# Attention and two MoE layers on one core: the third pair of heads of the first chunk through fp16 halves and DMA transposes, with a new order table

## The chip, the cores and the metric

The kernel runs on one core of one Trainium2 chip. The metric is the device time of the launch in microseconds (us), as a median over runs; lower is better. The five engines are named as the profile names them: PE is the matrix engine (PEld its weight loads), DVE the vector engine, ACT the scalar engine, POOL the GpSimd engine, SP the engine that issues most DMAs.

## What is computed

Attention with a hash mask, then two feed-forward layers, all in float32 at the interface. Batch 2, 8 heads, 768 positions, head size 64; the layers see 1536 tokens of width 512.

```python
def _attn_ref(q, k, v, proj):
    q_bits = (einsum(q, proj) > 0); k_bits = (einsum(k, proj) > 0)      # 6 bits -> a bucket
    mask = q_bucket[:, :, :, None] == k_bucket[:, :, None, :]
    scores = where(mask, scale * q @ k^T, -1e9)
    attn = exp(scores - max); attn = attn / (sum(attn) + 1e-09)
    return attn @ v
def _moe_ref(x, w1, w2, w3, w_out):      # d_ff 768
    return max(x @ w1, x @ w2, x @ w3) @ w_out
def _moe2_ref(x, w_in, w_out):           # d_ff 2048
    h = x @ w_in; g = where(h > 0, h, exp(min(h, 0)) - 1)
    return g @ w_out
```

## The kernel before

**Tiles.** The work is cut into six chunks of 256 tokens (c = 0 to 5; three for each batch), each chunk into four pairs of heads. A pair of a chunk is numbered u = 4c + p (24 of them), and is four tiles t = 4u to 4u + 3 (96 in all): two heads by two blocks of 128 queries, each against all 768 keys. For each tile `plan_tile` makes, in this chain: scores on PE (L621, four matmuls into one of the two PSUM tiles `s`), the row maximum on DVE (L624), two tiny DVE steps that make `scale` and `bias` (L625, L627), and the exponential on ACT into the float32 tile `P` (L629). Then P has to be transposed and multiplied with V, and there are two ways:

- **float32 path**, `if u < FU` with FU = 4, so all four pairs of chunk 0 (16 tiles). PE transposes P in six blocks back into the same `s` tile (L641, `turn32`), ACT copies that to SBUF (L645; the table may also give it to DVE), and PE multiplies in float32 with the raw V (L650, `pv32`; twelve matmul records for a tile). The row sum comes from the exponential itself, with an accumulate read behind it on ACT.
- **fp16 path**, all other pairs (80 tiles). P is split into two fp16 halves: a cast (L658 on ACT or L660 on DVE), the rest by a subtraction on POOL or DVE (L664), both into `hl`. SP issues a DMA transpose of twelve 128x128 blocks into `PT` (L666), and PE multiplies with V split likewise (L672 to L674, 18 matmuls). The row sum is a column of ones in V.

When the four tiles of a pair are done, L690 to L697 normalise them into `xn`, and after every second pair SP transposes `xn` into `xT` (L700), the input of the chunk's first layer.

**What else runs early.** `plan_qk` prepares q and k (load, norm, scaling L396 and L397, a split L398 and L400, PE transposes L410, copies to `qa`/`ka` L413, DMA copies to `qb`/`kb` L417, hash bits L429 to L464), `plan_v` prepares V, and `plan_w13` the weights of the first layer: loads into the three buffers `raww` (L531), conversions on ACT and DVE (L535, L539 or L540, L543 or L544, L546), a norm and a split (L558 to L560). The raw V of batch 0 lies in the space of `wot`, the second weight of the first layer; so `wot` is written after the last float32 product of chunk 0. The first layer (`plan_moe1`, L713) of a chunk starts when its `xT` is there; chunk 0's is the first large block of matmuls, and its second half (L713 with `wot`) needs the whole of the first half. The second layer (L713 with `win`, L848) follows.

**The order.** Nothing is scheduled at build time. `ORDER` is a packed table that lists all operations in one sequence with the engine of each; where an operation has two possible engines (a cast on ACT or DVE, a subtraction on POOL or DVE, a DMA issued from SP or ACT), the table chooses. Each engine carries out its own operations in that sequence, and waits at the head of it. Buffers of a ring are handed out in the same sequence.

Of the kernel before, what the change touches and what calls it, by code (L numbers as in the profile page):

```python
# [30 lines left out]
class Graph:  # L31
# [73 lines left out]
    "c-lQyOITXx))u_6@y5m*8*gm9vC$at$|h<6O~OWvfLG8cV48~QKx_wMG7y`A*bKyzf!Gejb|AI`@pK@z1F;>5?LbTiVmlB|2I9#;Ob3#a|9Sqk&H4Yezi)l-`>uDb4UgNcWz6SqKV$!(5=mvVN=j#N"  # L105
    "UYZxbaC_pfyb0VH#K#-Q{hL!L@yD)|EQI>ufz@F1o3Y)KSzPaUb6yn;&OCQ6#%A5uPUiA=F1Li6?m6)kt}A@s`|GDDxx3zQy0__k`*)Pktj44}ISg~}>3gp*<Qw!iGxo@|sC-`@Q!JXP_>nHIxOP*_"
    "Roys4;5BgO2-XzyrGa()oa>XK<R4~Lxc8|EI}ljad@;UnBlI%6^yj&H^Wo2!Qu8#Vo)4?^$Ajj`nQkc>NxwSwYa@oM^Xr)5<jv$~%S=CJet`#PhOHjtEoUn5s|h=ro!;|W@x8w$dEq%b?pO%!FK+mj"
    "jf9(3>+yuV&Mn`%EOrszj_*Z&R52#^FqUg;o{R3!U?F@3f8jFCi@%xwT^e?~E`Ih{CB%yjw?`r;HWya+13O+)9Xi;FD%7^{*}KR~Dzc`~z0$Q`gmw)Rp)0fPa^eU3kMZ}D_9eH>G2==2O1Y#N_D(NQ"
    "{-3qR1fAm-<E+zVUNIRQJF5tSPPn6-#a_?GyKM}!e7MHlfvrioIT+fb7@H?ZU;;hWJ?C4mt+orZpp1;$ncFtw<+JpFSRDMFm<%bcClb6`T6JbmVE&tOIQ7WV(BJ3^3sVZe4L;_e;zK$1Lmh4ttHao-"
    "?r68UmJ`Jd5!Ibqk(n2qpcb^!_PJO{WD|xB&z72xH_uRW#4X{!u*Rp5W&E4f8O9g07oIP#7ffC+xv8jq=kr^acNEcp?ZA$IKzVx}bx8c%OI$vGqMMu}V&*?wYf|r}L+&<DM?P$L3|k4#^*LqdKUC`Y"  # L110
    "{DrS$g0ZmfUqt+i+(2&}^Bu$z74DgD#;K##F{AER+s2=p>|=v#-C~b8u$?yx*XB~+p`P)I`60@6ZT@PlKKlANwu2oEBH@2du+YeN=Letr&-wlUH;DYAeSWkWGf3WFGxwJni70YLoJ;WqvPvm8Cs;jG"
    "u9Nyp<;=gltn?Wl6^ifdeu*02vV!7uJ}P)A(XeJqi3u4z0^vneY%W~2oeerJS9F}c=>N=zH>AIj2xYE4vu<PW7XQGVE{q5WKln*m?V!@Fx3x#tf+}KW)lk>zF?oNSQ^n-I!*lP1ukA;FLhM4ecN}+r"
# [861 lines left out]
```

## Time and profile before

| | |
|---|---|
| three runs | 646.3, 646.44, 650.33 us; median 646.44 |
| the profiled execution | 646.06 us, of which 644.3 us from the first to the last instruction |
| mean granted clock of PE | 0.997 of full speed |
| busy, share of the span | PE 97%, DVE 82%, ACT 71%, POOL 34% |
| DMA | 81.35 MB, mean 126 GB/s |

The profile is one execution. Busy shares are averages over stages with different limits: the first 140 us (attention of chunk 0, preparing of weights, the first layer of chunk 0) look otherwise than the rest, so the stretches are read one by one. A row of the timeline has the start, the duration, the engine, the line, the operation and its tiles, and in brackets the idle time before it with what ended that. A matmul's row lasts from its issue to the modelled end of its pipeline; the next may start long before that, so the step from start to start is what it takes of PE.

### The profile page before, as it was taken

What the parts mean: (1) busy time and instruction counts of PE and PEld (TensorE: products, weight loads), DVE (VectorE), ACT (ScalarE), POOL (GpSimd) and SP (SyncE); (2) the same over time, 40 slices, a digit from 0 to 9 for tenths busy, and PEclk for the clock granted to TensorE, in tenths of its full rate; (3) what the DMA queues carried; (4) which work ended last, traced back from release to release, by engine and by line L of the source; (5) the groups of instructions that cost most, each with busy time, mean ns of one, the idle gap of its engine ahead of it and who ended that gap; (6) DMA issues with size and microseconds to landing.
All of it is one profiled execution on the core that took longest, in us unless ns stands there. A gap on an engine that the chain in (4) does not pass through costs nothing.

```text
span 644.3 us, 16489 instructions
## 1 busy us (share of the span) xinstructions
PE 624.7 (97%) x6414; PEld 490.8 (76%) x6414; DVE 528.0 (82%) x1493; ACT 454.8 (71%) x858; POOL 218.5 (34%) x196
## 2 busy tenths in 40 slices
PE   4999889999999999999999999999999999999997
PEld 4788768888888888888888887766676666667664
DVE  6899999998878988898765898888888676887564
ACT  3899999999878777866635878866755665554431
POOL 1210175756656474575631101112111221120021
PEclk9999989999999999999999999999999999999999
DMA  8775699979799777888666634231302100000022
GB/s 261 200 242 152 180 202 229 217 131 218 150 189 178 149 156 164 174 169 151 147 132 218 181 96 128 68 99 35 97 19 71 45 1 2 1 1 2 1 92 105
DMA packets 176030, 81.35 MB, mean 126 GB/s; under 512 B 142672, under 2 KB 170320, under 8 KB 175952
## 3 DMA queue, kind: packets, MB, share of 16 engines
q1 hardware_dynamic: 171678, 75.54, 50.3%
q10 hardware_dynamic: 4274, 4.76, 2.6%
q8 instruction: 50, 0.82, 0.6%
q14 instruction: 28, 0.23, 0.1%
HBM read 38.80 MB, written 3.15 MB: 65 GB/s over the span
## 4 chain that ended last, share of the span: by engine, by line
PE 80%; DVE 4%; ACT 4%; DMA 3%; issue 1%; POOL 0%; DVEq 0%; SPq 0%; ACTq 0%
PE mo L713 47%; PE out L848 19%; PE s L621 6%; PE o L672 2%; PE o L673 2%; PE o L674 2%; ACT P L629 1%; DVE m L624 1%; DMA kb<-ka 1%; DMA rawv<-in_v_dram 1%; PE mo L410 1%; DMA PT<-hl 1%; ACT hl L645 1%; DVE hx L734 0%; ACT mo L535 0%
## 5 line engine op out<-in xcount | busy, mean ns | idle before, releaser
L713 PE MATMUL mo<-xT,w 128*128 128x256 f16 x1296 | 152.6, 272 | 0.0
L664 POOL TENSOR_TENSOR hl<-P,hl 128x768 f16<-128x768 f32 x69 | 115.0, 1674 | 64.9 <-ACT hl L658 31.5
L713 PEld LDWEIGHTS <-w 128*128 128x128 f16 x1296 | 123.6, 98 | 16.7
L713 PE MATMUL mo<-x1T,win 128*128 128x256 f16 x1152 | 135.8, 273 | 0.0
L848 PE MATMUL out<-wo2t,gt 128*128 128x512 f16 x576 | 134.9, 379 | 0.0
L713 PEld LDWEIGHTS <-win 128*128 128x128 f16 x1152 | 112.3, 98 | 24.2
L629 ACT ACTIVATE P<-s,bias,scale 128x768 f32<-128x768 f32 x96 | 94.6, 991 | 28.8 <-DVE bias L627 17.6
L841 POOL TENSOR_TENSOR gt<-g,gt 128x256 f16<-128x256 f32 x57 | 39.3, 695 | 213.2 <-ACT gt L839 125.4
L624 DVE TENSOR_REDUCE m<-s 128x1 f32<-128x768 f32 x96 | 91.1, 951 | 12.6 <-PE s L621 11.2
L848 PEld LDWEIGHTS <-gt 128*128 128x128 f16 x576 | 54.9, 97 | 52.7
L832 ACT ACTIVATE r<-mo,nih 128x256 f32<-128x256 f32 x96 | 44.8, 469 | 69.1 <-PE mo L713 65.0
L835 DVE TENSOR_SCALAR uu<-e,sg 128x256 f32<-128x256 f32 x96 | 35.5, 371 | 26.3 <-ACT e L834 25.7
L658 ACT CAST hl<-P 128x768 f16<-128x768 f32 x62 | 50.7, 830 | 2.9 <-DMA PT<-hl 2.4
L672 PE MATMUL o<-vt,PT 128*128 128x65 f16 x480 | 51.3, 193 | 0.2
L673 PE MATMUL o<-vt,PT 128*128 128x64 f16 x480 | 51.3, 194 | 0.0
L674 PE MATMUL o<-vt,PT 128*128 128x65 f16 x480 | 51.1, 192 | 0.0
L837 DVE SCALAR_TENSOR_TENSOR g<-mo,aj,uu 128x256 f32<-128x256 f32 x96 | 46.1, 482 | 6.0 <-POOL gt L841 2.0
L621 PE MATMUL s<-ka,qa 128*128 128x384 f16 x192 | 48.1, 332 | 2.5 <-ACT P L629 1.9
L621 PE MATMUL s<-kb,qb 76*128 76x384 f16 x192 | 48.2, 332 | 1.0 <-DMA kb<-ka 1.0
L672 PEld LDWEIGHTS <-PT 128*128 128x128 f16 x480 | 44.4, 96 | 2.7 <-DMA PT<-hl 0.4
L673 PEld LDWEIGHTS <-PT 128*128 128x128 f16 x480 | 44.3, 97 | 2.1
L713 PEld LDWEIGHTS <-wot 128*128 128x128 f16 x432 | 41.4, 98 | 5.6
(212 smaller groups left out, 1158.7 us busy)
## 6 DMA issues: line engine op xcount, KB each, us to landing
raww<-in_moe_w_dram SPq DMA_DIRECT2D x17, 512.0 KB
raw<-in_moe_w_in_dram SPq DMA_DIRECT2D x14, 512.0 KB
raw<-in_moe_w_out_dram SPq DMA_DIRECT2D x13, 512.0 KB
rawk<-in_k_dram SPq DMA_DIRECT2D x8, 384.0 KB
raww<-in_moe_w_out_dram SPq DMA_DIRECT2D x6, 512.0 KB
out_dram<-ot SPq DMA_DIRECT2D x12, 256.0 KB
rawq<-in_q_dram SPq DMA_DIRECT2D x10, 256.0 KB
wot<-in_v_dram SPq DMA_DIRECT2D x4, 384.0 KB
```

What stands on the lines that cost most here:

```text
L621: PE.matmul(ps.ap[:, h, :NK], lh[0:n, h0 + i, j], rh[0:n, i, h * CH:(h + 1) * CH], start=first, stop=not first)
L624: op({"V": vred(S)}, lambda e: V.tensor_reduce(out=m.ap, in_=ps.ap[:, :, :NK], op=ALU.max, axis=AX.XY), rd=[ps], wr=[m], prio=t + 80.5)
L629: op({"A": act(S, ap=2, acc=int(u < FU)) - 42}, lambda e: A.activation(out=P.ap.rearrange("p (c n) -> p c n", c=2), in_=ps.ap[:, :, :NK], ...
L658: A.copy(hl.ap[:, 0], P.ap)
L664: op({"G": gtt(S), "V": (vtt(S), -109.46)}, lambda e: eng[e].tensor_tensor(out=hl.ap[:, 1], in0=P.ap, in1=hl.ap[:, 0], op=ALU.subtract), r ...
L672: PE.matmul(oo, pt.ap[:, kt], vt.ap[:, i, kt, :D + 1], start=(kt == 0), stop=False)
L673: PE.matmul(oo[:, :D], pt.ap[:, kt], vt.ap[:, i, kt, D + 2:], start=False, stop=False)
L674: PE.matmul(oo, pt.ap[:, NS + kt], vt.ap[:, i, kt, :D + 1], start=False, stop=(kt == NS - 1))
L713: PE.matmul(o, lh(kk, x), rh(kk, y), start=(kk == 0 and pi == 0), stop=(kk == n - 1 and pi == 2))
L832: op({"A": act(NQ, ap=1) - 42}, lambda e, m=m, o=o, r=r: A.activation(out=r.ap, in_=o.ap[:, :NQ], func=AF.Relu, scale=nih.ap[:, m:m + 1]), ...
L837: op({"V": vstt(NQ)}, lambda e, m=m, o=o, uu=uu, gg=gg: V.scalar_tensor_tensor(out=gg.ap, in0=o.ap[:, :NQ], scalar=aj.ap[:, m:m + 1], in1= ...
L848: PE.matmul(outs[j].ap, gt.ap[:, x, j * 128:(j + 1) * 128], wo2t[f].ap[:, y], start=(len(seen) == 1 and pi == 0), stop=(len(seen) == n and ...
```

## The change

The tiles of u = 2 (t = 8 to 11, the third pair of chunk 0) go by the fp16 path; u = 0, 1 and 3 stay in float32. Every `u < FU` becomes `u in FS`. The cost entries of three DMA operations change by a unit or take other numbers; `emit` does not read them. ORDER is a new table, for 3363 operations where there were 3359.

```diff
 ORDER = (
-    "c-lQyOITXx))u_6@y5m*8*gm9vC$at$|h<6O~OWvfLG8cV48~QKx_wMG7y`A*bKyzf!Gejb
...
+    "c-l2qOI#Xv*A~2SQ@LpvyfJuVP$M8JU^If42pR=M19)S+Bx1S{zjq<F3$a}U+lAOH#C9Pz3
...
-FU = 4
+FS = (0,1,3,)
...
-            if u < FU:
+            if u in FS:
                 plan_tile.zs = tn(UL, "zs", 2)
...
-        pt = ring(at, [128, 2 * NS, 128], "PT", 4, F16, True) if u >= FU else None
+        pt = ring(at, [128, 2 * NS, 128], "PT", 4, F16, True) if u not in FS else None
...
-            **(dict(accum_out=zs.ap[:, j * 2 + i:j * 2 + i + 1]) if u < FU else {})),
-           rd=[ps, sc, bi], wr=[P] + ([zs] if u < FU else []), prio=t + -196.32)
+            **(dict(accum_out=zs.ap[:, j * 2 + i:j * 2 + i + 1]) if u in FS else {})),
+           rd=[ps, sc, bi], wr=[P] + ([zs] if u in FS else []), prio=t + -196.32)
...
-        if u < FU:
+        if u in FS:
...
             def turn32(e):
...
-        if u >= FU:
+        if u not in FS:
             op({"A": act(S), "V": (vcopy(S), 337.62)}, hi, rd=[P], wr=[hl], two=True, prio=t + 53.24)
...
-        if u >= FU:
+        if u not in FS:
             attn_ops.append(op({"PE": 3 * pe(NS, D + 1)}, pv, rd=[pt, vt], wr=[o], prio=t + 7.27 + -25.59))
```

What the new table does with u = 2 shows on three engines. First ACT, at the tiles of u = 2. Before, two exponentials (with their row sums `zs`) and two copies of the transposed tile, with weight work (`dc2w`, `w`) between:

```order
L629 ACTIVATE P_1238,zs_1114<-s_1179,bias_1221,scale_1211 128x768
L558 ACTIVATE w_100<-dc2w_1029,swm 128x512
L543 ACTIVATE dc2w_1133<-raww_927 128x512
L629 ACTIVATE P_1261,zs_1114<-s_1205,bias_1252,scale_1247 128x768
L645 COPY hl_1268<-s_1179 128x768
L539 ACTIVATE dc2w_1277<-raww_1146 128x512
L645 COPY hl_1288<-s_1205 128x768
```

Now, at the same place:

```order
L629 ACTIVATE P_1123<-s_1075,bias_1102,scale_1089 128x768
L535 ACTIVATE mo_1127<-raww_1053 128x512
L629 ACTIVATE P_1132<-s_1084,bias_1116,scale_1114 128x768
L535 ACTIVATE mo_1146<-raww_1121 128x512
L658 CAST hl_1148<-P_1132 128x768
L413 COPY qa_1040<-mo_1039 128x1024
L629 ACTIVATE P_1181<-s_1135,bias_1144,scale_1142 128x768
```

The copies L645 are gone there, and of the four casts two stand on ACT (L658) and two on DVE (L660). Next POOL, from its third subtraction of k on. Before:

```order
L400 TENSOR_TENSOR natk_525<-rawk_247,natk_525 128x12x64
L400 TENSOR_TENSOR natq_646<-rawq_425,natq_646 128x8x64
L400 TENSOR_TENSOR natk_757<-rawk_416,natk_757 128x12x64
L400 TENSOR_TENSOR natq_1201<-rawq_764,natq_1201 128x8x64
L400 TENSOR_TENSOR natk_1286<-rawk_651,natk_1286 128x12x64
L697 TENSOR_TENSOR xn_1315<-xf_957,xn_1315 128x256
L697 TENSOR_TENSOR xn_1315<-xf_1216,xn_1315 128x256
```

Now:

```order
L400 TENSOR_TENSOR natk_693<-rawk_460,natk_693 128x12x64
L400 TENSOR_TENSOR natq_804<-rawq_517,natq_804 128x8x64
L400 TENSOR_TENSOR natq_1073<-rawq_960,natq_1073 128x8x64
L664 TENSOR_TENSOR hl_1125<-P_1123,hl_1125 128x768
L664 TENSOR_TENSOR hl_1148<-P_1132,hl_1148 128x768
L664 TENSOR_TENSOR hl_1214<-P_1181,hl_1214 128x768
L664 TENSOR_TENSOR hl_1239<-P_1237,hl_1239 128x768
L697 TENSOR_TENSOR xn_1217<-xf_987,xn_1217 128x256
L697 TENSOR_TENSOR xn_1217<-xf_1226,xn_1217 128x256
```

All four subtractions of u = 2 stand on POOL, ahead of the first `xn`; a k subtraction has left this place. Last SP, whose queue holds the loads of q, k and the weights and the copies to `kb` and `qb`. Before, from the copy of the fourth pair's keys on:

```order
L417 DMA kb3_845<-ka3_844 64x1536
L388 DMA rawq0_1235<-in_q_dram 128x4x128
L531 DMA raww1_1263<-in_moe_w3_dram 128x4x256
L464 DMA qb0_1050<-btq0_1177 12x8x128
L531 DMA raww0_1303<-in_moe_w1_dram 128x4x256
L388 DMA rawk0_1317<-in_k_dram 128x2x384
L531 DMA raww2_1391<-in_moe_w2_dram 128x4x256
L700 DMA_TRANSPOSE xT0_1407<-xn0_1315 128x8x128
```

Now, from the same copy on:

```order
L417 DMA kb3_758<-ka3_757 64x1536
L388 DMA rawq0_1192<-in_q_dram 128x4x128
L666 DMA_TRANSPOSE PT0_1199<-hl1_1125 128x12x128
L666 DMA_TRANSPOSE PT1_1234<-hl2_1148 128x12x128
L531 DMA raww2_1251<-in_moe_w1_dram 128x4x256
L666 DMA_TRANSPOSE PT2_1262<-hl0_1214 128x12x128
L666 DMA_TRANSPOSE PT3_1311<-hl1_1239 128x12x128
L531 DMA raww0_1426<-in_moe_w2_dram 128x4x256
L417 DMA qb0_1041<-qa0_1040 64x1024
L531 DMA raww1_1445<-in_moe_w2_dram 128x4x256
L464 DMA qb0_1041<-btq0_1406 12x8x128
```

Four transposes stand among the weight loads, and the loads of the fifth block of w1, w2 and w3 come behind them.

## Rows read from the trace of the kernel before

**Rows 1.** The page: span, busy time of PE, the chain by engine.

```profile
span 644.3 us, 16489 instructions
PE 624.7 (97%) x6414; PEld 490.8 (76%) x6414; DVE 528.0 (82%) x1493; ACT 454.8 (71%) x858; POOL 218.5 (34%) x196
PE 80%; DVE 4%; ACT 4%; DMA 3%; issue 1%; POOL 0%; DVEq 0%; SPq 0%; ACTq 0%
```

**Rows 2.** Stretches: length, busy us (instructions) by engine; PE clock, DMA share, GB/s.

```profile
40.00:60.00 20.00, 19.74 (x227) 17.74 (x226) 19.91 (x60) 20.00 (x37) 0.00 (x0) 1.00 0.60 182
60.00:80.00 20.00, 17.42 (x154) 14.95 (x152) 18.85 (x55) 19.22 (x37) 4.27 (x4) 1.00 0.65 177
80.00:100.00 20.00, 18.11 (x177) 14.50 (x175) 19.43 (x49) 19.87 (x29) 11.94 (x9) 0.91 0.96 193
100.00:120.00 20.00, 20.00 (x271) 16.94 (x267) 19.81 (x55) 20.00 (x32) 13.92 (x9) 1.00 1.05 237
0.00:139.50 139.50, 124.36 (x1479) 105.58 (x1480) 128.02 (x367) 125.81 (x214) 52.00 (x50) 0.99 0.83 206
139.50:640.50 501.00, 500.38 (x4937) 385.23 (x4934) 399.20 (x1126) 328.98 (x645) 166.46 (x146) 1.00 0.45 104
```

**Rows 3.** Timeline, PE: chunk 0's first product with wot.

```profile
139.51 0.82 PE L713 MATMUL mo<-hTa,wot 128*128 128x256 f16 x6
```

**Rows 4.** Timeline, PE: a float32 tile's transposes, its product, and what follows each.

```profile
56.81 0.87 PE L641 MATMUL s<-ident,P 128*128 128x128 f32 x6
57.52 0.22 PE L445 MATMUL mo<-ident,bitsq 128*96 128x128 f16 x1
...
58.23 1.45 PE L650 MATMUL o<-wot,hl 128*128 128x64 f32 x12
59.51 0.17 PE L280 MATMUL mo<-gm,ones 128*128 128x1 bf16 x1
```

**Rows 5.** Timeline, PE: first of 18 products of an fp16 tile, and what follows.

```profile
96.14 0.19 PE L672 MATMUL o<-vt,PT 128*128 128x65 f16 x1
...
96.68 0.49 PE L713 MATMUL mo<-xT,w 128*128 128x256 f16 x3
```

**Rows 6.** Groups by line: count, busy us, mean ns of one, idle before.

```profile
L645 ACT COPY hl<-s 128x768 f32<-128x768 f32 x16 | 12.6, 798 | 0.7 <-PE mo L281 0.7
L629 ACT ACTIVATION_READ_ACCUMULATOR P<-s,bias,scale 128x1 f32 x16 | 3.2, 203 | 0.0
L658 ACT CAST hl<-P 128x768 f16<-128x768 f32 x62 | 50.7, 830 | 2.9 <-DMA PT<-hl 2.4
L660 DVE CAST hl<-P 128x768 f16<-128x768 f32 x18 | 10.6, 588 | 0.1
L664 POOL TENSOR_TENSOR hl<-P,hl 128x768 f16<-128x768 f32 x69 | 115.0, 1674 | 64.9 <-ACT hl L658 31.5 <-DVE hl L660 18.0 <-issue 7.1
```

**Rows 7.** Timeline, DVE at the head: the first key norm.

```profile
7.31 0.29 DVE L301 TENSOR_REDUCE gm<-mo 128x1 f32<-128x128 f32 x1 [1.02 <-PE mo L297]
```

**Rows 8.** Tile PT: issue time on SP, min/median/max ns, first and last start.

```profile
L666 SPq DMA_TRANSPOSE PT<-hl x80: 1352/1414/3116, 86.2 to 329.3; - x80
```

**Rows 9.** Waits from 40 to 92 us: total, times, longest.

```profile
DVE dc2w L540 <- DMA raww<-in_moe_w_dram: 0.7, 1, 0.7
```

**Rows 10.** The chain in order of time: start, us, what.

```profile
60.60 6.27 DMA kb<-ka
```

**Rows 11.** Timeline: a DVE scaling that starts inside a POOL subtraction, and one alone.

```profile
80.33 0.42 DVE L398 TENSOR_SCALAR natq<-rawq 128x512 f16<-128x512 f32 x1
...
223.33 1.15 POOL L770 TENSOR_TENSOR x1T<-hx,x1T 128x512 f16<-128x512 f32 x1
...
223.49 1.28 DVE L398 TENSOR_SCALAR natq<-rawq 128x512 f16<-128x512 f32 x1
```

**Rows 12.** Stretches around the one fall of the granted clock.

```profile
85.00:86.00 1.00, 0.00 (x0) 0.00 (x0) 1.00 (x2) 1.00 (x3) 1.00 (x1) 1.00 0.57 121
86.60:90.00 3.40, 3.31 (x27) 2.40 (x27) 3.26 (x7) 3.37 (x5) 2.68 (x3) 0.53 1.15 210
```

More of the change, by code (lines that the diff above doesn't have):

```diff
@@ L109 @@
[L109 to L112, printed above, removed]
@@ new lines @@
+    "GV2e#dmU^;r;?adsn(`YSq95*-msxyesSM1dvtvEavtBdFCge;@Q;1>XUmDon=`W28)luy6T-+VOm`+_EVz}PHJo%?AW^OQeEt^Q`u4eekK_+<H-m9A9+M{mhmix-Y>@tU^6<BoDXrUe!W5AC0tfoQ"
+    "Ag1uKWfi8dNWD_!I$QIV+K)fK>1@%GjCkP8W<QM?Iw_Y9)?XT}aVFthw4BbHUL*}M3+Z}g0binib{zfr^g_R9`F1si#6xe7Y`FQrZi>uYZ`{~tqhx28=bA&;{_wf4kmP@Te*g2go<-(rBJc*;41BVD"
+    "HFR*e^A{SrrN}Ya7v6}%cM+ZOGj=qjgfDWjn>>iG`V17mTgZPAU>!yf^jGxlS9>9L=)D-zTX6e|>^vToDCZNucpGP5b|%|=Sj%rOv{ujj=X<NZn9bg1AXELEBQrka*Ujs{vj5b18gT4I3S3q^g-W(N"
+    "u=%k)$HKBVzBJE7?9Tlofn^;%#dLltuGEOXSW@v~XdL^(l(>~HAFDi3!_E6QDc09sDUIBM+jR~{mu2sC#~#Du2Wn>GcKL%>@3S*~jw=7sXJOH?l)UpPqEri_pE9sL-TAL^=@(PqCY1COu7jpIHT)!r"
@@ new lines @@
+    "vCdTv#o(_K2XR@aGqH4wy249(O;SWw`)6d@6|KcdLKas(9LM{1dEN~h?VFtkF4}d-y|V5POC#ICA#5tRun^+7&ZsW8?Qn^G^{?2n=jfHgyZYxwM1e*VvH7*q?+Sdft5u)cwHe)HiUY~*RKHfW6x=dc"
+    "L$;TQVE*sd-D4>BLr}IKSwg1lhia80W_8|po|Avxeh~?>kk+w(ed+NozU_YZ_Q+`G`EJmY&Fi0|;n>#F8HxqANmQ2f^W*4c;-55fEV@HkR>kMO_TK18)cvcOYu4_M-(u1wT}0hQQQ0X@%ZCu(6?O~Q"
+    "2Zt+aN5pV@#`K*3EJEf>OmRGs8exdY0((L7P`WHtUPLi9*|k2W(^vf-R9V#KKmT5*SeZCWsxuBs=C;;$9k|Oq;h|yh0WJ7LYYGJ24<B<dV_;29u`eA2Yd6A?f=yp{p+dmgIEcA?ZOHai^y0;*zgX}a"
+    ")c;x&_jtVGz2AJ>B<vIY)f)@E_U~_W)H7UfIX@u3+j4x<eHE5XIeGCkoRau}&Tg@$8{62JB5*@mlnOq>+{e+_%vi)pb5K;w>ytl_ufOe-#+itwOJNjXDLc|@<VR&#Gp#?3!FT)fzju=@I>W8`Q&h8^"
@@ new lines @@
+    "id&|FA^Z(RH{%Q+q9?9X7G|0;qZc2RE*WRe^}cHa6-$2K7JHavdiRi0nleQllC7*doa$-ULgQac<Q4Zi%eA$?>eCwiy8&LoH$j>8fBfOd;et@b4IT5M7jy1|=yuG}@{+>(^2502%4K_feM8a(|9tfx"
+    "edl#=ewL*E;vq$3I~xd<E%;<jS+&L7MNs|BVTkoXWSKe$`y!Y=<%dW#CR56Eh&g)Y7h-J_Z_TRGsZRXYF}uStzgXMqaJrTh3yRZL<b_)O<|KBy@}*v2aqh<OsfBnvmPo`6mf7pXKVE$GcH6z)jeW5s"
+    "Rd(-hPydgf6r|6acV8|~zr@qLs}7$g6n>=(!G6f>J3)3sL*dBzitrl|W$R4Jz4+|aO+f!=a^~{yv)`pYc<%my)8*EsIIkCYD^%}~`%KzjMz`n4i+pF>7-XLX(a`H7Ot#58M6pN<?{q6R!9&s7=x^_0"
+    "S7A*0gK8#;k*J*yj#crgs2R7bjQ_?Qvg@Ss=Iy)In4{ag-4bWrlC_4kd5djM{p+IUOS|jZwzj`1wL6@F;QEq3Uyt7|cD@XKZKP-qXM#>U+GRS5tUkBd|CP$v_4$uo?wkLtEQwP72!)4U2KFM-Go|<I"
@@ L153 @@
+    "YPAjzj#%#isl{d+g!2v-A{reW9UU4Pg6kt`vknao5y{ZtFu@L6M+b*Shix|75J3|G4#Ds+sD_EdhFfjJ0371s;gKPHa2OxNho23P4dWvt&xVHZk)h$yu`%1|<S>p8kKk}X1B8P(jt`CDV`KREI8OMn"
+    ";o%`0PT(#ZA15vxw@rM^$Hqp+?&$IHkqO|&CML$mC%{Zj+=ZYYp9BlxB*EX6#wRByCnhE*CJ8_Obn@vqkxx8*3fbgS0MQQhXJgMMA)kCo2%i#_$){t_o;`i~Z0aK>p56f>!aSS&7(W9{O@ae@eEd#G"
+    "FoXjQ*a<>mw*zN?3gd|Ee*ypQ8Bq"
 )
@@ L416, in plan_qk @@
         all_ = lambda t: t.ap.rearrange("p h s t -> p (h s) t")
-        op({"D": (475, 450, 1200 * (1 if kind == "k" else 0.75)), "A": (520, 460, 1200 * (1 if kind == "k" else 0.75), 341.16)}, lambda e: dq(e).dma_start(
+        op({"D": (475, 450, 1200 * (1 if kind == "k" else 0.75)), "A": (520, 460, 1201 if kind == "k" else 901, 341.16)}, lambda e: dq(e).dma_start(
             out=all_(tb)[0:64], in_=all_(ta)[hs * 64:hs * 64 + 64]), rd=[ta], wr=[tb], prio=prio + 433.29)
@@ L690, in plan_tile @@
         op({"V": TINY + 60}, lambda e: V.tensor_scalar(
-            out=z1.ap, in0=zs.ap if u < FU else o.ap[:, :, D], scalar1=1e-9, scalar2=vcr[:, 0:1] if u < FU else vmn[b][:, 2 + p:3 + p], op0=ALU.add, op1=ALU.mult),
-           rd=[zs, "vcr"] if u < FU else [o, f"vr{b}"], wr=[z1], two=u < FU, prio=pr + -112.32)
+            out=z1.ap, in0=zs.ap if u in FS else o.ap[:, :, D], scalar1=1e-9, scalar2=vcr[:, 0:1] if u in FS else vmn[b][:, 2 + p:3 + p], op0=ALU.add, op1=ALU.mult),
+           rd=[zs, "vcr"] if u in FS else [o, f"vr{b}"], wr=[z1], two=u in FS, prio=pr + -112.32)
         op({"V": TINY + 30}, lambda e: V.reciprocal(z.ap, z1.ap), rd=[z1], wr=[z], prio=pr + -235.05)
```

83 lines of the change are left out of this document (36 added, 47 removed).

## The prediction

> **What bounds the kernel now.** I read the page first, then the busy time by stretches, then the timeline at the places the change touches. On the page PE looks like the only bound: 97% busy and 80% of the chain [rows 1]. The stretches split that in two [rows 2]. From 139.5 us on, PE is busy 500.4 of 501.0 us, while DVE has a fifth of its time free and ACT a third: there PE alone sets the pace. Before that, three engines are full together. From 40 to 60 us ACT is busy 20.00 of 20 and DVE 19.91; from 60 to 80 ACT 19.22, DVE 18.85 and PE 17.42; from 80 to 100 ACT 19.87, DVE 19.43 and PE 18.11. The one with the most idle time in these stretches is PE, and its busy time flatters it: 18 matmuls whose rows last 0.19 us each follow one another in 0.54 us (96.14 to 96.68) [rows 5], so a stretch that is covered by rows need not be full. I read this as: until about 139.5 us, when PE begins chunk 0's product with wot [rows 3], DVE and ACT pace the kernel (weight preparing, maxima, exponentials, splits), and PE follows; afterwards PE paces it.
>
> That cut is chosen because everything of chunk 0's first layer has to be done at it, and because it lets the time be written as a sum: the moment of the cut, plus PE's work behind it. In both tables the same PE work stands behind the cut: 513 of PE's operations, of the same kinds. So with PE full there, what moves the end is what moves the cut.
>
> **The change part by part, PE.** Of a float32 tile, the six transposes take 0.71 us from start to start (56.81 to 57.52) and the product 1.28 us (58.23 to 59.51) [rows 4]. An fp16 tile's 18 products take 0.54 us [rows 5]. Four tiles change: 4 x (0.71 + 1.28 - 0.54) = 5.8 us of PE work go, all of it before the cut. If PE paced there, 5.8 us would be the gain. It does not, so I cost this at nothing: what hides it is the DVE and ACT work beside it. With that cover gone it is worth 5.8.
>
> **ACT and DVE, the exchange itself.** ACT loses four copies of 0.798 and four accumulate reads of 0.203, and gets two casts of 0.830; DVE gets two casts of 0.588 [rows 6]. That is ACT -2.3 us, DVE +1.2.
>
> **ACT and DVE, the new table.** The table shares all other work anew. Following the tiles back from the first product with wot, the order has 361 DVE operations that must be done before it in the old table and 368 in the new; on ACT 182 and 181. Counted kind by kind with the mean durations of the groups by line, DVE's list grows by 1.4 us (more hash-bit turns, word shifts, a subtraction, casts; fewer scalings and key copies), and ACT's too by 1.4 (the lost copies are paid back by scalings, a V split and casts taken over from DVE). For DVE the bounds are the exchange alone, +1.2, and seven operations at the mean of all before the cut, 128.02 / 367 = 0.35 us, so +2.4 [rows 2]. I take +1.4, the count by kind. If those engines keep their present idle time before the cut, it comes 1.4 us later.
>
> **Idle time before the cut.** DVE is idle for 139.5 - 128.0 = 11.5 us there [rows 2]. Some of that is the start, which nothing removes. One piece may go: DVE's 1.02 us before the first key norm [rows 7], as an early weight load, which ACT issues while the key loads are under way, is issued from SP behind the first V in the new table. Its price is between 0 and -1.0; I take 0, as one wait removed at the head is easily replaced by the next operand. Over all the idle time I allow 3 us either way for the forecast's own range, a little under half of what lies behind the first key norm.
>
> **POOL and SP.** POOL gets four subtractions of 1.674, 6.7 us [rows 6], at the tiles where it is now idle (0.00 of 20 us from 40 to 60, 4.27 from 60 to 80 [rows 2]); cost nothing, and if they wait, only `PT` of u = 2 is late, whose products share one `o` tile with u = 3. SP gets four transposes at 1.414 each, 5.7 us of issue time [rows 8], in front of the weight loads for the fifth block. I cost these at nothing too, since the loads wait for their three buffers anyway; the rival below says what it is if not.
>
> At one place a rule speaks against this. The Trainium skill, "VectorE: DVE Perf Modes", section "Rules for kernel authors", says to transpose on TensorE when a PSUM destination will do, and by DMA otherwise; the section "The three transpose paths" has 1309 ns for one 128x128 block by DMA. By that figure twelve blocks one after another would be an estimated 15.7 us for a tile. Here the issue takes 1.414 us [rows 8], and what the landing costs depends on whether PE has other work, which it has; the sum above stands without the page.
>
> **Sum.** Profiled execution 646.06 (span 644.3 and 1.8 around it) + 1.4 = 647.5 us. The median of the runs shown is 646.44, 0.4 above that execution, inside what one measurement gives. A change under about 1% (6.5 us) is what a measurement of this kernel can hardly tell from none.
>
> **Rivals.**
> *PE paces after all.* Then the 5.8 us come through: 640.3 us. For it: 97% on the page, 80% of the chain [rows 1], and a list of scores that starts as soon as an exponential frees one of the two `s` tiles; the fp16 path frees it after the exponential, the float32 path only after the copy. Against it: PE's idle time of 4.5 us from 60 to 100 us, while ACT lacks 0.9 there [rows 2]. Part of it could come, so 640.3 to 643.5.
>
> *Late weights (slower).* SP works in order. A transpose waits for its POOL subtraction, and every load and copy behind it waits too. If the four transposes delay the fifth block's loads by their full issue time, and DVE, which already waited 0.7 us for such a load [rows 9], waits as long, the cut comes 1.4 + 5.7 later: 653.2 us. For it: a copy of keys took 6.27 us from issue to landing on today's chain [rows 10], so SP's queue is able to hold the kernel up. Against it: the wait of 0.7 is the only one of DVE on a weight from 40 to 92 us. A delay costs from the first microsecond on, by that wait of 0.7; it makes the kernel slower by over 1% from 5.0 us on, so nearly the whole issue time of the four has to stand in the way.
>
> *POOL in DVE's way.* A DVE scaling that started 0.16 us into a POOL subtraction took 1.28 us instead of 0.42 [rows 11], so 0.86 more. With one such meeting for each of the four new subtractions, 646.06 + 1.4 + 3.4 = 650.9. Beside these rows stands the Trainium skill, "GPSIMD Engine Reference", section "Specifications": GpSimd's SBUF interfaces are shared with VectorE, with contention for certain DVE modes; the trace agrees for this pair. For it: the stretch where POOL is empty today is where DVE is fullest. Against it: the 18 casts L660 have a mean of 0.588 [rows 6], so few of them can have met one, and POOL is more than half busy from 80 us on [rows 2].
>
> *The clock.* PE stood still from 85 to 86 us, and from 86.6 to 90 its granted clock was 0.53 on average, near the 1.2 GHz level, instead of 1.00 [rows 12]. With 5.8 us less to do in a stretch where it waits already, PE may stand still once more; another 3.4 us at half clock cost up to 1.7 us of PE time: 649.2. Should the present fall vanish, it is 645.8. The second of these lies in the forecast's range.
>
> **Chances.** Forecast (cut moved by DVE and ACT, 644.5 to 650.5): 0.62. PE paces: 0.15. Late weights: 0.09. POOL meetings: 0.07. Clock: 0.07. The range of 8 in 10 goes from 641.5 to 652.5: it leaves out about half of "PE paces" and all of "late weights", together 0.17. Faster by over 1% (under 639.6 us) needs more than the whole PE saving: 0.04. Slower by over 1% (over 652.5) is the late weights: 0.09. Within 1%: 0.87.
>
> **What would show it.** In the changed kernel's profile: PE's first product with wot at 139.5 + 1.4 = 140.9 us; PE as good as full from there to the end, over 501 us; PE's steps per tile of u = 2 at 0.54 us and more PE idle time from 40 to 100 us, by about 5.8; DVE at 129.4 busy us before the cut; POOL with four L664 rows between 50 and 75 us. The forecast is wrong if the cut comes at 134 or before (PE or the `s` tiles paced), if DVE waits for `raww` for several us at the fifth block (late weights), if DVE rows of 1 us and more for L397, L398 or L660 stand beside the new POOL rows (meetings), or if a second stretch near half clock shows. It also fails if PE has more than 2 us of idle time behind the cut, since the sum takes that stretch as unchanged.

## The result, and the profile after

The changed kernel takes 652.93 us (median of 4 runs) where the kernel before takes 646.37; a repeat (e16) gave 653.55 against 646.17. The ratios are 1.0100 with a 95% interval of 1.0062 to 1.0137, and 1.0132 (1.0105 to 1.0158): about 1% slower. I had forecast 647.5 us, no change, and a range up to 652.5. The profiled execution after took 651.25 us with a span of 649.5, so 5.2 us of span are to be explained.

The page after (span, busy time of the engines, chain by engine and by line), beside [rows 1]:

```profile
span 649.5 us, 16505 instructions
PE 619.7 (95%) x6414; PEld 483.5 (74%) x6414; DVE 528.4 (81%) x1508; ACT 449.3 (69%) x845; POOL 216.2 (33%) x194
PE 63%; DVE 11%; DMA 10%; ACT 9%; issue 4%; POOL 2%; SPq 0%; DVEq 0%; ACTq 0%; POOLq 0%
PE mo L713 34%; PE out L848 19%; DMA PT<-hl 7%; PE s L621 4%; ACT P L629 2%; DVE m L624 2%; POOL hl L664 2%; PE o L672 1%; PE o L673 1%; PE o L674 1%; ACT hl L658 1%; ACT mo L535 1%; DMA rawv<-in_v_dram 1%; ACT junk L333 1%; DVE dc2w L546 1%
```

PE did 5.0 us less and the span grew. PE's part of the chain fell from 80% to 63%, and "DMA PT<-hl", the way of a tile through its DMA transpose, is a term of 7% where the old chain has 1%. (A share of the chain is not a wait: PE's waits follow below.) Chunk 0's first product with wot, which was at 139.51 [rows 3], is now at (timeline, PE):

```profile
137.69 0.82 PE L713 MATMUL mo<-hTa,wot 128*128 128x256 f16 x6
```

The stretches after, cut there as in [rows 2] (columns: length, busy us and instructions of PE, PEld, DVE, ACT, POOL, then PE clock, DMA share, GB/s):

```profile
40.00:60.00 20.00, 17.52 (x157) 14.63 (x156) 19.89 (x59) 20.00 (x35) 5.95 (x4) 1.00 0.67 179
60.00:80.00 20.00, 18.27 (x201) 15.02 (x200) 19.80 (x59) 19.92 (x35) 5.70 (x7) 0.91 1.06 230
80.00:100.00 20.00, 18.24 (x205) 14.63 (x205) 19.55 (x53) 19.97 (x31) 11.32 (x8) 1.00 1.00 216
0.00:137.69 137.69, 118.12 (x1480) 98.25 (x1480) 128.64 (x375) 126.38 (x209) 54.25 (x51) 0.99 0.90 220
137.69:645.70 508.01, 501.58 (x4936) 385.25 (x4934) 398.92 (x1134) 322.94 (x637) 161.91 (x143) 1.00 0.45 103
```

This gives the whole account. Ahead of the cut the changed kernel gains 139.51 - 137.69 = 1.8 us. Behind it, to PE's last matmul, it takes 508.0 us instead of 500.96: 7.05 us lost. Together 5.2. PE's busy time behind the cut is nearly the same (501.6 against 500.4); what is new is 6.4 us without any row, where there were 0.6. The waits of PE behind the cut up to 345 us (engine, line, releaser: us in all, times, longest), first of after, then all that the kernel before has:

```profile
PEld L621 <- issue: 2.9, 2, 1.8
PEld L672 <- DMA PT<-hl: 2.8, 3, 1.4
PE s L621 <- ACT P L629: 2.8, 2, 1.7
PE o L672 <- DMA PT<-hl: 2.4, 2, 1.3
```
```profile
PEld L281 <- issue: 0.8, 2, 0.6
PE mo L280 <- ACT junk L333: 0.5, 1, 0.5
PEld L672 <- DMA PT<-hl: 0.2, 1, 0.2
```

PE waits for transposed tiles (L672, at tiles 39 and 95) and for exponentials (L621, at tiles 71 and 92), far from the third pair's tiles 8 to 11. The edit of the path does not touch these; the new table does.

### The profile page after: what moved, and what is told of

It is laid out like the page before. It is cut to its first block, busy times and chain, and to the rows that moved or that the text cites. A ratio compares the mean times of both kernels' runs of the same rounds, so it can differ in the third digit from the quotient of the medians.

```text
span 649.5 us, 16505 instructions
## 1 busy us (share of the span) xinstructions
PE 619.7 (95%) x6414; PEld 483.5 (74%) x6414; DVE 528.4 (81%) x1508; ACT 449.3 (69%) x845; POOL 216.2 (33%) x194
## 4 chain that ended last, share of the span: by engine, by line
PE 63%; DVE 11%; DMA 10%; ACT 9%; issue 4%; POOL 2%; SPq 0%; DVEq 0%; ACTq 0%; POOLq 0%
PE mo L713 34%; PE out L848 19%; DMA PT<-hl 7%; PE s L621 4%; ACT P L629 2%; DVE m L624 2%; POOL hl L664 2%; PE o L672 1%; PE o L673 1%; PE o L674 1%; ACT hl L658 1%; ACT mo L535 1%; DMA rawv<-in_v_dram 1%; ACT junk L333 1%; DVE dc2w L546 1%
## 5 line engine op out<-in xcount | busy, mean ns | idle before, releaser
L664 POOL TENSOR_TENSOR hl<-P,hl 128x768 f16<-128x768 f32 x74 | 123.2, 1671 | 88.7 <-ACT hl L658 47.6
L672 PE MATMUL o<-vt,PT 128*128 128x65 f16 x504 | 54.4, 194 | 4.3 <-DMA PT<-hl 3.0
L658 ACT CAST hl<-P 128x768 f16<-128x768 f32 x62 | 51.2, 831 | 5.6 <-DMA PT<-hl 5.2
L673 PE MATMUL o<-vt,PT 128*128 128x64 f16 x504 | 54.3, 195 | 0.0
L674 PE MATMUL o<-vt,PT 128*128 128x65 f16 x504 | 54.2, 194 | 0.0
L621 PE MATMUL s<-ka,qa 128*128 128x384 f16 x192 | 47.1, 327 | 6.5 <-ACT P L629 5.5
L672 PEld LDWEIGHTS <-PT 128*128 128x128 f16 x504 | 46.9, 97 | 6.7 <-DMA PT<-hl 4.8
L673 PEld LDWEIGHTS <-PT 128*128 128x128 f16 x504 | 46.9, 98 | 2.9 <-issue 1.2
L621 PE MATMUL s<-kb,qb 76*128 76x384 f16 x192 | 47.1, 326 | 0.4 <-DMA kb<-btk 0.4
L674 PEld LDWEIGHTS <-PT 128*128 128x128 f16 x504 | 47.0, 99 | 0.0
```

The lines of the kernel that those rows point to most:

```text
L621: PE.matmul(ps.ap[:, h, :NK], lh[0:n, h0 + i, j], rh[0:n, i, h * CH:(h + 1) * CH], start=first, stop=not first)
L658: A.copy(hl.ap[:, 0], P.ap)
L664: op({"G": gtt(S), "V": (vtt(S), -109.46)}, lambda e: eng[e].tensor_tensor(out=hl.ap[:, 1], in0=P.ap, in1=hl.ap[:, 0], op=ALU.subtract), r ...
L672: PE.matmul(oo, pt.ap[:, kt], vt.ap[:, i, kt, :D + 1], start=(kt == 0), stop=False)
L673: PE.matmul(oo[:, :D], pt.ap[:, kt], vt.ap[:, i, kt, D + 2:], start=False, stop=False)
L674: PE.matmul(oo, pt.ap[:, NS + kt], vt.ap[:, i, kt, :D + 1], start=False, stop=(kt == NS - 1))
```

## The experiments

In each, "cut" is the start of the first product with wot, and "behind" the time from there to PE's last matmul, read from the profile as above. For orientation, all that were made to locate the loss (us; the ratio is to the kernel before on the same chip):

| kernel | median | ratio (95%) | cut | behind |
|---|---|---|---|---|
| before | 646.4 | | 139.51 | 500.96 |
| changed | 652.9 | 1.010 (1.006 to 1.014) | 137.69 | 508.01 |
| changed, repeat (e16) | 653.6 | 1.013 (1.011 to 1.016) | 139.21 | 507.96 |
| e1: old table, fp16 path | 653.1 | 1.011 (1.008 to 1.015) | 144.40 | 502.26 |
| e2: new table, float32 path | 661.9 | 1.023 (1.021 to 1.026) | 148.28 | 507.69 |
| e3: new table, PE's order mended | 653.4 | 1.011 (1.006 to 1.015) | 141.00 | 509.70 |
| e4: old table to 220 us, then new | 650.6 | 1.008 (1.005 to 1.011) | 138.19 | 506.85 |
| e5: new table to 126 us, then old | 646.4 | 0.999 (0.997 to 1.002) | 139.41 | 501.32 |

> The changed kernel once more, on the chip of the three runs beside it: 651 to 655 us in all and 507 to 509 us behind the cut, as in its first profile, if that stretch is a property of the table and not of one execution.

The repeat says how far to trust these columns: "behind" came back within 0.05 us, the cut within 1.5. So "behind" goes with the table, and the cut has a scatter of 1 to 2 us between executions. Each row is one profile, though: the runs with the old order behind the cut (before, e1, e5, and e11 and e12 below) lie between 500.65 and 502.41, so a difference under 2 us says little.

**Path or table (e1, e2).** The change is two things, so I did each alone.

```diff
 e1:  FS = (0,1,3,)   ORDER: new -> old, with hi, lo, transpose and product of u = 2
                      where its copies and products stood, and some operations next to them
 e2:  FU = 4          ORDER: old -> new, with transposes, copy and product of u = 2
                      where hi and product stand
```

> The third pair (u = 2) goes through the fp16 path as in the changed kernel, but all other work keeps the order and the engines of the old table: the hi casts stand on ACT where the float32 copies stood, then the POOL subtraction and the SP transpose; the four products, the normalizing of u = 2, and the first two products of u = 3 stand a few places later. Theory 'table' (the loss of 6.5 us is in the new order of the work behind 100 us, not in the path): 643 to 649 us, PE's waiting behind 100 us at most 5 us as in the kernel before. Theory 'path' (the four POOL subtractions, SP transposes and what they delay cost the time): 651 us or more.

> The reverse: the new table, with u = 2 back on the float32 path (transposes on PE, copy on the engine that had the cast, float32 product; no POOL subtraction and no SP transpose for u = 2). Theory 'table': 652 to 658 us, no better than the changed kernel, since PE gets its 5.8 us of work back and the waits behind 100 us stay. Theory 'path': back to 645 to 648 us.

The medians support neither theory alone: the path with the old table costs 6 us, and the new table without the path costs 15. The column "behind" sorts it: 502.3 with the old table and 507.7 with the new, whatever the path. The path's cost in e1 is nearly all ahead of the cut (144.40), where PE stood and its granted clock then fell to near 1.2 GHz (columns as above):

```profile
50.00:60.00 10.00, 7.47 (x72) 6.33 (x71) 9.96 (x20) 9.00 (x15) 4.45 (x2) 1.00 0.68 194
60.00:70.00 10.00, 6.53 (x52) 3.89 (x51) 10.00 (x22) 8.88 (x15) 4.96 (x3) 0.53 0.91 225
70.00:80.00 10.00, 7.89 (x79) 6.95 (x79) 8.58 (x27) 6.27 (x12) 3.10 (x3) 0.62 0.84 227
```

DVE is full there and PE half idle. The timeline shows what fills DVE (the line numbers of e1 are lower by one):

```profile
55.35 4.45 POOL L663 TENSOR_TENSOR hl<-P,hl 128x768 f16<-128x768 f32 x2 [19.11 <-ACT hl L657]
55.91 2.40 DVE L501 SCALAR_TENSOR_TENSOR vt<-wot,vs,vt 128x768 f16<-128x768 f32 x1
58.23 1.88 DVE L539 TENSOR_SCALAR dc2w<-raww 128x512 uint16<-128x512 uint16 x1
60.58 0.16 PE L279 MATMUL mo<-gm,ones 128*128 128x1 bf16 x1 [2.85 <-DVE gm L300]
```

The four new POOL subtractions stand at 55.4 to 59.8 and 65.5 to 69.3, and each holds up one DVE operation: these two, which take 1.01 and 0.46 us where no POOL operation meets them, and two more at 66.57 (1.27 instead of 0.48) and 67.76 (1.90 instead of 0.46). That is 5.0 us together. DVE does 367 operations ahead of the cut before and in e1, and is busy 128.0 us with them before and 133.3 in e1; the cut comes 4.9 us later. This is the rival that I had called "POOL in DVE's way". PE's stop and the low clock follow it in time; what the clock costs by itself was not separated. Where the moved operations of u = 2 stand in e1 and e2 was my choice, so their heads say nothing on the best that either combination could do.

**PE's own order (e3).**

```diff
 ORDER: 18 of PE's operations behind 95 us moved by 1 to 5 places in PE's order, such as
-  product of P, tile 39 | sum of squares of the keys
+  sum of squares of the keys | product of P, tile 39
```

> The changed kernel with 18 of PE's operations behind 100 us moved by one to five places in PE's own order (a product with a transposed P, scores, a first-layer product put behind or ahead of neighbours that are ready); every other engine and every queue keeps its sequence, and the fp16 path of u = 2 is as in the changed kernel. Theory 'table': PE's order has products too close behind what they wait for, so 3 to 5 us of the 13 us of waiting behind 100 us go, 648 to 650 us. Theory 'path' (or a slower engine behind PE): the waits move to the next operation, 652 to 654 us.

653.4 us, 509.7 behind the cut: nothing recovered. PE's idle time behind the cut is 7.0 us here, where it was 6.4, so the waits moved on. My reading, not tested apart: the tiles' buffers and the other engines' sequences stay as they are, and they set when PE's next operand comes.

**Where in the table (e4, e5).**

```diff
 e4:  ORDER: old[first 1354 operations] + the rest as in new   (float32 path)
 e5:  ORDER: new[first 784 operations] + the rest as in old    (fp16 path, seam smoothed)
```

> The kernel before (float32 path for all four pairs) with its own table up to about 220 us, and the rest of the work in the order and on the engines of the new table. Theory 'table', read from the two traces: behind 220 us PE waits 5 us more in the changed kernel than before, so 650 to 652 us. If it comes out at 645 to 648, the new table loses its time ahead of 220 us alone, and the later waits are what the earlier ones leave behind.

> The changed kernel up to about 126 us (fp16 path for u = 2, new order and engines), and everything behind it in the order and on the engines of the old table, with some of the 130 operations behind the seam moved by a few places to fit. Theory 'tail' (the new table's head is 2 to 7 us ahead on PE, as its first products show, and its order behind the cut loses 5 to 7 us again): the head's gain stays, 640 to 645 us, with PE as good as full behind 130 us. Theory 'debt' (the head is ahead on PE only because it puts work of other engines off, and any order has to pay for it behind): PE waits behind 126 us with the old order too, 649 to 654 us.

e5 is level with the kernel before: with the old order behind 126 us the loss is gone (501.3 behind the cut), with path and head of the changed kernel in place. So the loss is settled as the new table's order (sequence and choice of engines) behind the cut. e4 has 506.85 with only the stretch from 220 us on new, so 5.9 of the 7.05 us arise there, if the seam costs nothing; in the changed kernel's own profile 4.9 of the 6.4 us of idle PE time behind the cut lie behind 220 us. But e5 did not come out at 640 to 645 either: the head's lead on PE (its tiles of u = 4 start some 5 us earlier than before) is gone at the cut, 139.41.

**Rearranged tables (e6 to e8) and mixtures (e9, e10).** I tried to mend the order on all engines, placing the operations one behind another with the durations of the traces' rows.

```diff
 e6:  ORDER of changed, all engines' sequences between 100 and 420 us rearranged, engines kept
 e7:  the same over the whole kernel
 e8:  ORDER of before, rearranged over the whole kernel
 e9:  changed, but behind 126 us each operation on the engine of the old table
 e10: e5, but behind 126 us each operation on the engine of the new table
```

> The changed kernel with the same head up to about 100 us and every operation on the same engine; behind that the sequences of PE, DVE, ACT, POOL and the SP queue up to about 420 us are rearranged so that fewer operations wait for a late one. Theory 'tail': most of the 13 us of PE waiting behind 100 us go, 638 to 646 us. Theory 'debt': the work put off is the same, so 649 us or more, with DVE or ACT full where PE waits.

> As the run with the rearranged tail, but with the head rearranged as well (fp16 path for u = 2, engines of all operations as in the changed kernel). If waits set by the order are what is lost, 634 to 642 us; if the head's pace is set by the engines' work, no better than the run with the rearranged tail.

> The kernel before (float32 path for all four pairs, engines as in the old table) with its order rearranged in the same way and with the same effort. If the path of u = 2 itself brings its 5.8 us of PE work once no order stands in the way, this run is 4 to 8 us slower than the rearranged changed kernel; if the path brings nothing (its gain is hidden by DVE and ACT in the head), both come out within 3 us.

> The changed kernel with its own sequence throughout, but behind about 126 us every operation on the engine that the old table gives it (272 operations change between ACT, DVE and POOL or between the ACT and SP queues); ahead of 126 us as in the changed kernel. From the first product with wot to the end the kernel before takes 501.0 us and the changed kernel 508.0. Theory 'sequence' (the new order itself stands too close to what it waits for): 506 to 512 us behind the cut, 650 to 656 in all. Theory 'engines' (which engine does what, with POOL or ACT too late): 501 to 503 behind the cut, 645 to 648 in all. Theory 'fit' (sequence and engines belong together): worse than both, 655 us or more.

> The counterpart: the new head up to 126 us, then the old sequence, but with the engines of the new table. Theory 'sequence': 501 to 503 us behind the cut, 645 to 648 in all, as with the old engines. Theory 'engines': 506 to 510 behind the cut, 650 to 654 in all. Theory 'fit': 655 us or more.

All five are far slower: 665.7 (ratio 1.031, 1.029 to 1.034), 684.4 (1.059), 687.3 (1.063), 696.7 (1.077) and 675.6 (1.044). My placing had left out that DVE and POOL hold each other up. e6 has the same operations on the same engines as the changed kernel, yet DVE is busy 16 us more and POOL 6 more than in the page above. How much of e6's lost time this is was not tested:

```profile
PE 626.2 (94%) x6414; PEld 485.8 (73%) x6414; DVE 544.4 (82%) x1508; ACT 448.7 (68%) x845; POOL 222.1 (33%) x194
```

e9 and e10 share one head and exchange order and engines behind it. Either mixture is much worse than either table, 547.6 and 532.1 us behind the cut, which is the theory "fit": a table's sequence and its choice of engines hold for each other, and neither can be judged or mended alone. e7 and e8 came out 2.9 us apart, within the 3 us expected if the path brings nothing, but two tables so far from the originals do not decide it.

**What paces the head (e11, e12).**

```diff
 e11 (before), u = 2 only:
-   for kt in range(NS):   # transposes and float32 products
+   for kt in range(1):
 e12 (e5), the 24 tiles of w1, w2, w3 and wo:
-   A.activation(out=t1.ap, ...)       V.scalar_tensor_tensor(out=t2.ap, ...)
+   A.activation(out=t1.ap[:, :256], ...)  V.scalar_tensor_tensor(out=t2.ap[:, :256], ...)
```

> The kernel before, with one of six transposes and one of six products in each tile of u = 2 (the attention of the third pair leaves out five of six key blocks): 4 x 5/6 x (0.71 + 1.28) = 6.6 us less PE work in the head, everything else the same. Prediction's reading (DVE and ACT pace the head, PE follows): the first product with wot comes within 1.5 us of 139.3, the whole within 3 us of the kernel before. If PE paces: 5 to 6.6 us earlier, 640 us.

> The kernel with the new head up to 126 us and the old order behind it (646.35 us), with two operations of each of the 24 weight tiles of the first layer and wo on half of their columns (the ACT scaling of 0.63 us and the DVE combination of 0.68 us; half of these weights' words are left out): about 5 us less on ACT and 6.5 on DVE, nearly all of it ahead of the cut. Prediction's reading (DVE and ACT pace the head): the cut comes 4 to 6 us earlier than 139.2, and the whole takes 640 to 643 us. If PE or the chain of a tile paces: the cut within 1.5 us, 645 us or more.

e11: 646.9 us, ratio 1.0001 (0.9974 to 1.0027). PE had 6.6 us less to do in the head and the kernel took the same time (cut 137.78, within the scatter). e12: 644.3 us, 0.995 (0.992 to 0.998), with the cut 2.8 us earlier than in e5. First e5's stretch up to the cut, then e12's:

```profile
0.00:139.41 139.41, 119.68 (x1479) 99.39 (x1480) 129.46 (x373) 127.54 (x210) 55.25 (x52) 0.98 0.88 217
```
```profile
0.00:136.57 136.57, 118.69 (x1480) 98.73 (x1480) 123.44 (x373) 123.02 (x210) 55.92 (x52) 0.99 0.89 221
```

DVE had 6.0 and ACT 4.5 us less to do; the cut came 2.8 us earlier, where I had expected 4 to 6, and the end 2.0. That agrees with DVE and ACT pacing the head, with about half of what is taken off them coming through, but 2.8 is not far above the scatter of the cut. A run made for another question, e15 (next part), speaks against DVE alone: with the maxima halved DVE has 8.6 us less to do ahead of the cut than in e16 (120.4 against 128.9), ACT nearly the same, and the cut comes no earlier than in e16 (139.21):

```profile
0.00:141.00 141.00, 120.57 (x1479) 99.55 (x1480) 120.37 (x377) 126.92 (x209) 54.76 (x51) 0.96 0.87 215
```

In that execution the granted clock also fell, to 0.66 from 80 to 90 us, so it is not a clean test. That PE does not pace the head is shown by e11; what paces it is not shown to the end.

**Which link is late behind the cut (e13 to e15, e17).**

```diff
 e14:
-   SP.dma_start_transpose(out=pt.ap, in_=hl)                       # 12 blocks
+   SP.dma_start_transpose(out=pt.ap[:, :NS], in_=hl[:, S//2:3*S//2])  # 6 blocks, each used twice
 e13: e14, and the subtraction L664 on half of its columns
 e15: V.tensor_reduce(max) over ps[:, 1] instead of ps[:, :]
 e17: e14's edit in the kernel before
```

> The same with whole subtractions: only the SP transposes are halved (6 of 12 blocks). If the DMA transposes are the link that is late, 504 us or less behind the cut, near the run with both halved; if POOL is, 506 us or more here and 504 or less there; theory 'front': 506 or more in both.

> The changed kernel; in every tile on the fp16 path the SP transpose moves 6 of 12 blocks and the POOL (or DVE) subtraction makes half of the low columns (the products take each transposed block twice, so half of the keys' probabilities are left out; PE's work is the same). Theory 'link' (the 7 us behind the cut are waits at the end of a tile's chain, through subtraction and transpose): behind the cut 503 us or less instead of 508.0. Theory 'front' (the waits start at the scores: maximum, exponential and what stands before them on DVE and ACT): 506 us or more behind the cut.

> The changed kernel with the maximum of each tile over one of the two halves of its scores (the other half of the keys is left out of the maximum): the DVE reduction of 0.95 us becomes about 0.55 in all 96 tiles, so DVE has 0.4 us per tile less and the exponential can start 0.4 us earlier. Theory 'front': behind the cut 504 us or less. Theory 'link': 506 us or more, though the cut itself may come up to 6 us earlier, since DVE has 13 us less to do ahead of it.

> The control: the kernel before with the same halved SP transposes (6 of 12 blocks in each of its 80 fp16 tiles; half of the keys' probabilities left out). The changed kernel lost 8.4 us by this, 4.5 of them behind the cut. If the new order is what stands close behind the transposes, the old one gains at most 2 us behind the cut (PE waits 2.5 us there in all) and at most 3 us in all. If transposes hold both tables up alike, 6 to 8 us in all.

| kernel | median | ratio to before (95%) | behind |
|---|---|---|---|
| changed (e16, same chip as the next three) | 653.6 | 1.013 (1.011 to 1.016) | 507.96 |
| e14: transposes halved | 645.2 | 0.999 (0.996 to 1.002) | 503.48 |
| e13: transposes and subtractions halved | 643.5 | 0.996 (0.994 to 0.998) | 502.11 |
| e15: maximum halved | 652.1 | 1.010 (1.007 to 1.013) | 505.64 |
| e17: before, transposes halved | 645.2 | 0.997 (0.994 to 0.9995) | 499.79 |

Halving the transposes takes 8.4 us off the changed kernel and 2.4 off the kernel before, and both then take 645.2 us. Behind the cut it is 4.5 us against 1.2, so the transposes carry 3.3 of the 7.05 us there, about half; the rest of the 8.4 lies ahead of the cut, where executions scatter by 1 to 2 us. Halving the subtractions brings 1.4 more behind the cut and halving the maxima 2.3 (e15 lies between the bounds of my two theories); both are near the spread of that column, and the medians move by 1.7 and 1.4. So the DMA transpose is the largest link found, and not the only one. Of the 6.4 us of PE's idle time behind the cut 2.8 are left in e14, and PE's waits for transposes are all but gone:

```profile
PEld L672 <- DMA PT<-hl: 0.2, 1, 0.2
```

It isn't that the new table puts products nearer to their transposes: from issue to product the 63 tiles behind the cut take 8.1 us in the median before and 7.8 after, and 13 of them are under 6 us in both. It is a few places where other work stands ready too late. The largest wait of PE is one of those that stay. It shows how a transpose reaches PE through ACT (timeline of after; the bracket is the idle time before the row and what ended it):

```profile
238.96 10.29 SPq L666 DMA_TRANSPOSE PT<-hl  x4
249.30 1.58 SPq L700 DMA_TRANSPOSE xT<-xn  x1
```
```profile
250.78 0.83 ACT L658 CAST hl<-P 128x768 f16<-128x768 f32 x1 [1.93 <-DMA PT<-hl]
...
251.52 0.99 ACT L629 ACTIVATE P<-s,bias,scale 128x768 f32<-128x768 f32 x1
...
252.55 0.48 PE L621 MATMUL s<-ka,qa 128*128 128x384 f16 x2 [1.72 <-ACT P L629]
```

Four transposes follow one another on SP from 239 to 249 us, three of which start as their subtraction ends. ACT's cast needs a free `hl` buffer, which the transpose of an older tile gives back; the exponential stands behind that cast on ACT; PE's scores need the `s` buffer that the exponential gives back. In e14, with half the blocks, the same two rows are:

```profile
247.09 0.83 ACT L658 CAST hl<-P 128x768 f16<-128x768 f32 x1 [1.91 <-DMA PT<-hl]
248.87 0.49 PE L621 MATMUL s<-ka,qa 128*128 128x384 f16 x2 [1.50 <-ACT P L629]
```

So the size of the transposes is not what makes this place late; when they can start, and the order of the work around them, may be. A place of the other kind is at 311.51, where DVE meets a POOL subtraction:

```profile
311.22 1.76 POOL L664 TENSOR_TENSOR hl<-P,hl 128x768 f16<-128x768 f32 x1 [0.69 <-ACT hl L658]
311.51 2.02 DVE L745 TENSOR_TENSOR hTb<-hx,hTb 128x512 f16<-128x512 f32 x1
313.52 0.94 DVE L624 TENSOR_REDUCE m<-s 128x1 f32<-128x768 f32 x1
```

The split of hTb takes 2.02 us where one that meets no POOL operation takes 0.69, the maximum of tile 91 begins that much later, and the scores of the next tile wait 1.0 us. This wait stays in e14. Of the 7.05 us, 3.7 remain between e14 and e17. PE's idle time behind the cut, 2.8 us against 0.1, is most of that, and these two places are 2.5 of it; I did not take them away one by one.

## Why the prediction was wrong

**The step that failed** is "in both tables the same PE work stands behind the cut ... so with PE full there, what moves the end is what moves the cut". The work is the same; PE was not full. From the count of operations (513 of PE's in both tables, which holds) I took a stretch of 501 us as unchanged, in a table that gives them new places. What the runs showed in its place: with the new order behind the cut PE stands idle for 6.4 us there, waiting for transposed tiles and exponentials, and with the old order put back (e5) for 0.8. The term belongs in the sum as +7.05 us. I had written down that more than 2 us of idle PE time behind the cut would break the sum, and gave no chance to it; with bounds for it, slower by over 1% could not have stood at 0.09.

**The cut.** Forecast 140.9; measured 137.69, 139.21 in the repeat and 139.41 in e5. The first is 3.2 us off, a little more than the 3 us allowed, the others less; all three on the other side. DVE's busy time ahead of it was 128.64 us for the 129.4 forecast. The +1.4 is smaller than the scatter and neither shown nor refuted.

**PE's 5.8 us cost at nothing.** Right. e11 takes 6.6 us off PE in the old table, to no effect; e5, with a new head besides, has that saving in it and is level with the kernel before. "PE paces" (640.3) falls. The sign that I had named for it did not come: PE's idle time from 40 to 100 us grew by 1.2 us and not by 5.8, since other work moved up into the stretch (scores of u = 4 start some 5 us earlier). That DVE and ACT are the cover agrees with e12 for about half of what was taken off them; with e15 beside it, it is not shown.

**POOL and SP at nothing.** Right for the changed kernel's head: the four new subtractions stand between 53.5 and 62.5 us, and DVE waits for no weight load from 40 to 100 us. With the old table the same path cost 5 us at the cut (e1), by the meetings with DVE and what followed them, so "nothing" holds for the table that was made for it.

**Late weights.** Its time, 653.2, is nearly what was measured, and its mechanism is absent: PE begins the first product with wot earlier, not 7 us later. A rival is judged by its place in the trace, not by its sum. The Trainium skill, "DMA: Bandwidth & Descriptors", section "Rules for kernel authors", says to issue a transfer early and to wait on it late, so that its fixed cost overlaps with compute. No run here tests that rule: from issue to product the two tables leave a transpose the same time in the median (8.1 and 7.8 us).

**Meetings of POOL and DVE.** In the changed kernel not where I looked for them: inside the four new subtractions no DVE row is held, and the six casts L660 ahead of the cut have a mean of 552 ns (588 in [rows 6]). One of the waits behind the cut is such a meeting. In e1 the rival happened as I had priced it, one meeting for each of the four subtractions, 5.0 us where I had 3.4; so the new table's head avoids what the old order runs into. **The clock.** The granted clock of the whole execution is 0.997 before and after, so it explains nothing of the difference; in e1 it fell as well (0.53 from 60 to 70 us), behind PE's stop.

**The transposes' own time.** The figure that I quoted from the Trainium skill, "VectorE: DVE Perf Modes", section "The three transpose paths", was 1309 ns for one block, and 15.7 us for twelve in a row was my estimate from it. That sum does not hold here: the first product follows the issue by 3.8 us at the earliest after the change. The waits that cost the time are on tiles that went by the fp16 path before, too, so it is the new order around their transposes that failed to cover them, and not the exchanged path of u = 2.

## What to carry to other kernels

When a hand-tuned order table is replaced, cost the whole table, not the stretch that the edit touches: here a stretch without idle time lost that property with a new order of the same work. Compare "from here to the end" in two profiles before explaining medians; here one subtraction of two rows located 7 us that the two medians, the path and the head had mixed up. And to test whether a latency limits a table, shorten it in both tables: 8.4 us against 2.4 says that it does, and the waits that stay say where it does not.

## What the runs showed of the hardware

The time in which SP is held by a DMA transpose hardly follows its size (tile PT: count, min/median/max ns): 12 blocks in the changed kernel, then 6 in e14.

```profile
L666 SPq DMA_TRANSPOSE PT<-hl x84: 1277/1432/3828, 55.3 to 332.6; - x84
```
```profile
L666 SPq DMA_TRANSPOSE PT<-hl x84: 1209/1218/2279, 58.1 to 328.9; - x84
```

Half the blocks save 0.2 us of issue. From issue to landing no row tells; the product follows the issue at the earliest by about the same time with 12 blocks and with 6 (3.65 us before, 3.78 after, 3.75 in e14). The halving also freed room in the DMA queues (DMA share behind the cut 0.45 to 0.34), for the other transfers too; whether that or the transposes' own landing brought the gain was not taken apart.

A DVE operation with all its operands in SBUF that starts inside a POOL operation is often held until shortly before that one ends: above, POOL ends at 312.98, and 313.53 less the usual 0.69 is 312.84. The maxima, which read PSUM, stay at 0.95 us under POOL. Taking the tenth percentile of a line's rows as its usual time, the DVE rows that start inside a POOL TENSOR_TENSOR take 22.7 us more than usual in the changed kernel and 42.5 in e6, and the other rows about 8 us in both. So the 16 us by which DVE is busier in e6 are such meetings.
